# A sixteen-row piece more kept in SBUF by a two-pass channel gate, with the raw rows loaded and stored in another order

## The chip, the cores and the metric

The kernel runs on one core of one Trainium2 chip. The time is the device time of an execution in microseconds; of several runs the median counts. Shares, stretches and chains of waits come from one profiled execution.

## The reference

`x` is 1 x 384 x 384 x 384 in bf16 (113 MB), `w1d` a single weight.

```python
g = jnp.einsum("bhwc->bc", x) / (H * W)      # mean of each channel
s = sigmoid(g * w1d[0])                      # with k = 1 the window is one channel wide
return x * s[:, None, None, :]
```

Every output element needs the mean over the whole input, so `x` is gone through twice: once for the sums, once for the product. It does not fit on the chip.

## The kernel before

**Rows.** A row is one vector of 384 channels in each of the 128 partitions: 768 bytes per partition, 98,304 bytes in all. The input is 1152 rows. One tile, `arena`, holds 275 rows; everything is loaded into it, changed in place and stored from it.

**Kept and streamed rows.** In pass one all 1152 rows are loaded and summed. 785 of them are streamed: summed, overwritten, and loaded again in pass two. 367 are kept in `arena` until the gate is known, more than it has rows, since most are folded: the values of `x` lie in a range in which four exponent bits of each bf16 word are the same in all of them, and the bits of a fourth row are spread over these places in three others. A group of q quads takes 4q loaded rows, of which 3q stay (`GROUPS`, line 168: one of 4, eight of 8 in two columns, and `BANKED`, line 174, of 6, whose folded rows are put into PSUM). 296 kept rows are folded and 71 are raw (`N_RAW`, line 177). A group is worked in pieces of at most 4 quads (`PIECE`), which is 16 rows.

**Fold and unfold.** `fold` (line 292) of a piece first tests the exponent bits: DVE writes the test into scratch Y and ACT sums it into `seen`. Then DVE shifts fields of the fourth row into scratch T and joins them to the three others. Two tests, one after the other, use the same Y. `unfold` (line 470) rebuilds the fourth row with scratch Y in `fields`, restores and scales the three in `three`, and scales the fourth in `fourth`. If a test ever failed, GpSimd would redo the folded rows (`again`, line 540); the trace shows no such work.

**The arena's places.** The two columns of groups, with U (8 rows) and V (8 rows) behind them, which hold the fourth rows of the last groups during the fold; then A, 39 rows, used as three slots S1, S2, S3 of 13 rows; then T (8 rows) and Y (8 rows), the scratch. U, V, the 39 rows of A, T and Y take raw rows at the end of pass one.

**Engines and queues.** SP issues every load and store of rows, in the order of the program, and waits in that order. PE sums rows by a matmul with ones (`sum_rows`, line 253). DVE folds, unfolds and scales; GpSimd scales 13 raw rows in three instructions behind the gate. `Flow` (line 21) gives each operation the waits that its reads and writes of rows demand; a load waits for the sums or stores of what it overwrites.

**End of pass one.** For each group in turn (`BETWEEN`, line 404, and the loop behind it), its rows are loaded, folded and summed while streamed rows pass through the places that are still free, at last through the slots. Then come the raw rows: S2, U, S3, S1, V, Y, and T in two parts. The gate follows on ACT (line 443) and is copied to PSUM for DVE.

**Pass two.** A planner in Python (from line 564) walks a model of the engines in steps of 0.05 us and so fixes the order: which rows DVE scales or unfolds next (`landed`, `turns`), when a store is issued, and when the rows freed by a store are loaded again (`runs`). `landed` starts with the raw rows in a fixed order (line 620): Y, U, T, V, S1, S2. The groups are unfolded in the order `order` (line 634). A group may start when the scratch and its column's places have been stored (`needed`, line 607). Rows of Y, U and V are not given to loads once they are stored, the others are (line 615).

Of the kernel before, what the change touches and what calls it, by code (L numbers as in the profile page):

```python
# [127 lines left out]
def kernel(  # L128
# [25 lines left out]
    PIECE = 4  # L154
    PAIR = 2 * PIECE
    PAIRS = 4
    U = 3 * PIECE + PAIRS * 3 * PAIR
    G0 = U + PAIR
    V = G0 + PAIRS * 3 * PAIR
    A = V + PAIR  # L160
    N_A = 39
    T = A + N_A
    Y = T + 2 * PIECE
    ROWS = Y + 2 * PIECE
# [3 lines left out]
    GROUPS = [(0, PIECE)]  # L168
# [4 lines left out]
            GROUPS.append((a + 3 * PAIR * i, PAIR))  # L173
    BANKED = len(GROUPS)
    GROUPS.append((A, 6))
    PS = 3 * GROUPS[BANKED][1]
    N_RAW = ROWS - V + PAIR
    pool = ctx.enter_context(tc.tile_pool(name="sb", bufs=1))
    psum = ctx.enter_context(tc.tile_pool(name="psum", bufs=1, space=bass.MemoryType.PSUM))

# [15 lines left out]
    BANK = nc.PSUM_BANK_SIZE_BYTES // 2  # L196
    banks = [psum.tile([P, BANK], bf16, name=f"bank{i + 1}") for i in range((PS * C + BANK - 1) // BANK)]

# [6 lines left out]
    def rows(lo, n):  # L205
        return [("a", r) for r in range(lo, lo + n)]
# [4 lines left out]

    N_STREAM = RPP - N_RAW - sum(4 * q for _, q in GROUPS)
    N_KEPT = RPP - N_STREAM
    assert N_STREAM % 2 and N_KEPT % 2
    STREAMED, KEPT = (0, N_STREAM), (N_STREAM, N_KEPT)
# [5 lines left out]
    c_raw = r  # L221
    assert r + N_RAW == N_KEPT

    def raw(a):

        return c_raw + (a - U if a < G0 else PAIR + a - V)


    summed = [0]
# [1 line left out]
    def load(chunk, a, lo, hi):  # L231

        r0, n = chunk
        fl.add(
            "SP",
            lambda: nc.sync.dma_start(out=arena[:, a : a + hi - lo, :], in_=view(xf, r0, n)[:, lo:hi, :]),  # L236
            writes=rows(a, hi - lo), dma=True,
        )
# [14 lines left out]
    def sum_rows(a, n):  # L253
        def emit(i, first, last):
            if first:
                return nc.tensor.matmul(acc, lhsT=ones[:], rhs=arena[:, i, :], start=first, stop=last)  # L256
            return add_held(arena[:, i, :], last)

        for i in range(a, a + n):
            first, last = summed[0] == 0, summed[0] == RPP - 1  # L260
            fl.add(
                "PE", lambda i=i, f=first, l=last: emit(i, f, l),
                reads=[("a", i), "ones"], writes=["bank0"],
            )
            summed[0] += 1
# [7 lines left out]
    def bits(dst, src, op0, s0, op1, s1, reads, writes):  # L273
        fl.add(
            "DVE",
            lambda: nc.vector.tensor_scalar(out=dst, in0=src, scalar1=s0, scalar2=s1, op0=op0, op1=op1),  # L276
            reads=reads, writes=writes,
        )

    def join(dst, a, b, op, reads, writes):  # L280
        fl.add(
            "DVE", lambda: nc.vector.tensor_tensor(out=dst, in0=a, in1=b, op=op), reads=reads, writes=writes  # L282
        )

    def flat(a, p):
        return arena[:, a : a + p, :].bitcast(u16)
# [5 lines left out]
    def fold(k):  # L292

        g, lo, p = pieces[k]
        first, q = GROUPS[g]
        a, ua = first + 3 * lo, first + 3 * q + lo
        wc = [rows(a + j * p, p) for j in range(3)]
        u, uc = flat(ua, p), rows(ua, p)
        t, tc2 = flat(T, 2 * p), rows(T, 2 * p)

        def field(i, op, by, mask):
            bits(flat(T + i * p, p), u, op, by, AND, mask, uc, rows(T + i * p, p))

        def test(i, parts):

            at = Y
            for first, n in parts:
                bits(flat(at, n), flat(first, n), AND, 0x7800, XOR, 0x3800, rows(first, n), rows(at, n))
                at += n
            y = flat(Y, 2 * p)  # L310
            fl.add(
                "ACT",
                lambda: nc.scalar.activation(  # L313
                    out=y, in_=y, func=ACTF.Copy, accum_out=seen[:, 2 * k + i : 2 * k + i + 1]
                ),
                reads=rows(Y, 2 * p), writes=rows(Y, 2 * p) + [("seen", 2 * k + i)],
            )

        test(0, [(a, 2 * p)])
        field(0, SHL, 4, 0x7800)  # L320
        field(1, SHL, 8, 0x7800)
        w01 = flat(a, 2 * p)
        join(w01, w01, t, XOR, wc[0] + wc[1] + tc2, wc[0] + wc[1])
        test(1, [(a + 2 * p, p), (ua, p)])
        field(0, SHL, 12, 0x7000)
        field(1, SHR, 4, 0x0800)
        w2 = flat(a + 2 * p, p)
        for i in range(2):
            join(w2, w2, flat(T + i * p, p), XOR, wc[2] + rows(T + i * p, p), wc[2])
# [17 lines left out]
    streamed = [0]  # L347
# [3 lines left out]
    def stream(n, a):  # L351
        load(STREAMED, a, streamed[0], streamed[0] + n)
        if n > 40 and folding:
            keep_warm(N_WARM)
        sum_rows(a, n)
        streamed[0] += n

    def stream_all(where, n=None):
        i = 0
        n = sum(m for _, m in where) if n is None else n  # L360
        while n:
            a, m = where[i % len(where)]
            m = min(n, m)
            stream(m, a)
            n -= m
            i += 1

    def take(g, lo=0, hi=None):

        a, q = GROUPS[g]  # L370
        hi = 4 * q if hi is None else hi
        load(KEPT, a + lo, c_group[g] + lo, c_group[g] + hi)
        sum_rows(a + lo, hi - lo)

    def of_group(g):
        return [i for i, piece in enumerate(pieces) if piece[0] == g]
# [3 lines left out]
    for k in of_group(BANKED):  # L380
        fold(k)
    in_arena = arena[:, A : A + PS, :].rearrange("p r c -> p (r c)")

    def copy_bank(i, src, dst, reads, writes):
        fl.add(
            "ACT", lambda: nc.scalar.copy(dst.bitcast(u32), src.bitcast(u32)), reads=reads, writes=writes  # L386
        )

    for i, bk in enumerate(banks):
        lo, hi = i * BANK, min((i + 1) * BANK, PS * C)  # L390
        copy_bank(i, in_arena[:, lo:hi], bk[:, 0 : hi - lo], rows(A, PS), [("bank", i)])

    SLOTS = [(A + i, 13) for i in range(0, N_A, 13)]
    S1, S2, S3 = ([slot] for slot in SLOTS)
# [8 lines left out]
    BETWEEN = [  # L403
        LOW_COLUMN, HIGH,
        LOW_COLUMN, [(A, 39)],
        [(G0 - 24, 24), (A - 24, 24)], (S1, S2 + S3),
        (S1, S2 + S3 + S1), (S2, S3 + S1),
    ]
    between = sum(n for b in BETWEEN for w in b for _, n in (w if isinstance(w, list) else [w]))
    first = N_STREAM - between  # L410
    stream_all(EARLY[3:], first % 48)
    stream_all(EARLY, first - first % 48)
# [3 lines left out]
    for g, where in zip(range(1, BANKED), BETWEEN):  # L416
# [6 lines left out]
        else:  # L423
# [4 lines left out]
            take(g, 12, 24)  # L428
            fold(k2)
            stream_all(where[1])  # L430
    assert streamed[0] == N_STREAM

    def take_raw(a, n):
        load(KEPT, a, raw(a), raw(a) + n)
        sum_rows(a, n)

    for a, n in S2 + [(U, 8)] + S3 + S1 + [(V, 8), (Y, 8), (T, 5), (T + 5, 3)]:
        take_raw(a, n)
    assert summed[0] == RPP

# [131 lines left out]
    landed = deque()  # L572
# [31 lines left out]


    SCRATCH = rows(Y, 8)
    needed = [set(SCRATCH + rows(U, 8)), set(SCRATCH + rows(V, 8)), set(SCRATCH)]

    def stored(a, n):

        def f():
            for i in range(a, a + n):
                for left in needed:
                    left.discard(("a", i))
                if not Y <= i < Y + 8 and not U <= i < U + 8 and not V <= i < V + 8:
                    idle[i] = True
        return f


    for a, n, end in ((Y, 4, True), (Y + 4, 4, True), (U, 4, True), (U + 4, 4, True), (T, 8, True), (V, 8, True)):  # L620
        landed.append((KEPT, a, raw(a), n, end))
    for a, n in SLOTS[:2]:
        landed.append((KEPT, a, raw(a), n, True))


    alongside = deque()
# [4 lines left out]
        alongside.append((t, KEPT, a, raw(a), n))  # L631


    order = [g for i in (3, 2) for g in (1 + 2 * i, 2 + 2 * i)] + [BANKED]
    order += [g for i in (1, 0) for g in (1 + 2 * i, 2 + 2 * i)] + [FIRST]
    line = deque(order)
    home = {g: i for i, column in enumerate(COLUMNS) for g in column}
    home[BANKED] = 2
    free = [True, True, True]
    total = len(GROUPS)  # L640
    out_rows = 0
    turns = deque()
# [45 lines left out]
    while True:  # L688

        if dve_at <= now:  # L690
# [4 lines left out]
            if landed and (ahead < PENDING or not can):  # L695
                chunk, a, lo, n, end = landed.popleft()
# [3 lines left out]
                if end or ahead < MERGE:  # L700
                    b, first = since
# [8 lines left out]
        if alongside and alongside[0][0] <= now:  # L710
            _, chunk, a, lo, n = alongside.popleft()
            store(chunk, a, lo, lo + n)
            moves.append([now + LAT, n * ROW + PER_STORE, stored(a, n)])
        while waiting and waiting[0][0] <= now:
            _, n, then, chunk, a, lo, known = waiting.popleft()
# [11 lines left out]
        got = runs()  # L727
        if bank_at is None and len(line) <= total - BANKS_AT and got and max(got)[0] >= PS * 4 // 3:
            a = max(got)[1]
            for i in range(a, a + PS * 4 // 3):  # L730
                idle[i] = False
# [7 lines left out]
        if got and todo < N_STREAM:  # L739
            n, a = max(got)  # L740
            n = min(n, CAP, N_STREAM - todo)
# [52 lines left out]
```

## Time and profile before

| what | value |
|---|---|
| median of 3 runs | 720.82 us (720.63 to 722.88) |
| span of the profiled execution | 719.4 us |
| bytes read / written in HBM | 190.41 / 113.25 MB |
| share of the 16 DMA engines' time taken by packets | 99.0% |
| end of the last sum, gate, first store issued | 268.1, 268.1 to 268.7, 269.7 us |

The span runs from the first to the last instruction of the core; what lies around it, the launch, is not in the trace. The strip over the span shows 40 slices of 18 us: tenths busy for DVE and DMA, and GB/s.

```
DVE  4600004788999719988999998999998985095500
DMA  9999999999999979999999999999999999999997
GB/s 379 435 433 435 426 428 435 438 434 425 426 426 429 427 326 376 421 391 423 430 430 437 430 428 441 428 433 435 430 436 433 429 437 428 441 432 427 440 439 314
```

Slices 15 and 16 hold the seam between the passes. A stretch of the span, as shown further down, can be read for each engine's busy time and for what the DMA engines moved; the chain of waits names, from the end back, what released each step.

### The profile page before, as it was taken

What the parts mean: (1) busy time and instruction counts of PE and PEld (TensorE: products, weight loads), DVE (VectorE), ACT (ScalarE), POOL (GpSimd) and SP (SyncE); (2) the same over time, 40 slices, a digit from 0 to 9 for tenths busy, and PEclk for the clock granted to TensorE, in tenths of its full rate; (3) what the DMA queues carried; (4) which work ended last, traced back from release to release, by engine and by line L of the source; (5) the groups of instructions that cost most, each with busy time, mean ns of one, the idle gap of its engine ahead of it and who ended that gap; (6) DMA issues with size and microseconds to landing.
All of it is one profiled execution on the core that took longest, in us unless ns stands there. A gap on an engine that the chain in (4) does not pass through costs nothing.

```text
span 719.4 us, 2061 instructions
## 1 busy us (share of the span) xinstructions
PE 213.0 (30%) x1202; PEld 0.3 (0%) x3; DVE 493.9 (69%) x471; ACT 115.7 (16%) x93; POOL 10.6 (1%) x7
## 2 busy tenths in 40 slices
PE   4677788897987770000000000000000000000000
PEld 0000000000000000000000000000000000000000
DVE  4600004788999719988999998999998985095500
ACT  3600003566677610002000000000000000000000
POOL 0000000000000005000000000000000000000000
PEclk9899999999999995555555555555555555555555
DMA  9999999999999979999999999999999999999997
GB/s 379 435 433 435 426 428 435 438 434 425 426 426 429 427 326 376 421 391 423 430 430 437 430 428 441 428 433 435 430 436 433 429 437 428 441 432 427 440 439 314
DMA packets 20174, 303.79 MB, mean 422 GB/s; under 512 B 2243, under 2 KB 2243, under 8 KB 6083
## 3 DMA queue, kind: packets, MB, share of 16 engines
q1 hardware_dynamic: 20160, 303.67, 99.0%
q8 instruction: 4, 0.07, 0.0%
q14 instruction: 8, 0.06, 0.0%
q10 hardware_dynamic: 2, 0.00, 0.0%
HBM read 190.41 MB, written 113.25 MB: 422 GB/s over the span
## 4 chain that ended last, share of the span: by engine, by line
DMA 63%; DVE 23%; PE 6%; ACT 2%; another core or an unknown queue 1%; SPq 1%; issue 0%; DVEq 0%
DMA arena<-in_x_dram 42%; DMA out_dram<-arena 20%; DVE arena L456 16%; PE bank L242 6%; DVE arena L276 4%; DVE arena L282 3%; ACT arena L313 2%; SPq L236 1%; ACT s_bf L443 0%; SPq L789 0%; DVEq L112 0%; SPq L106 0%
## 5 line engine op out<-in xcount | busy, mean ns | idle before, releaser
L456 DVE TENSOR_TENSOR arena<-arena,s_bf 128x4608 bf16<-128x4608 bf16 (+8 forms) x97 | 228.7, 2390 | 68.2 <-DMA arena<-in_x_dram 52.2
L276 DVE TENSOR_SCALAR arena<-arena 128x1536 uint16<-128x1536 uint16 (+2 forms) x247 | 145.3, 633 | 111.6 <-DMA arena<-in_x_dram 101.8
L242 PE MATMUL bank<-arena,ones 128*128 128x384 bf16 x1151 | 204.6, 339 | 46.3 <-DMA arena<-in_x_dram 46.3
L313 ACT ACTIVATE arena<-arena 128x3072 uint16<-128x3072 uint16 (+1 forms) x38 | 102.4, 2696 | 142.1 <-DVE arena L276 142.1
L282 DVE TENSOR_TENSOR arena<-arena 128x1536 uint16<-128x1536 uint16 (+2 forms) x114 | 121.0, 1061 | 5.2 <-PE bank L242 2.8
L529 PE MATMUL bank<-odd,ones 128*128 128x1 bf16 x1 | 0.2, 187 | 322.6 <-DVE odd L524 322.6
L456 POOL TENSOR_TENSOR arena<-arena,s_bf 128x1536 bf16<-128x1536 bf16 (+1 forms) x3 | 10.4, 3481 | 268.7 <-ACT bank L447 268.7
L386 ACT COPY arena<-bank 128x512 uint32<-128x512 uint32 (+1 forms) x7 | 4.0, 570 | 58.2 <-DMA out_dram<-arena 58.1
L456 DVE TENSOR_TENSOR arena<-arena,bank 128x1536 bf16<-128x1536 bf16 (+2 forms) x7 | 11.3, 1689 | 0.0
L242 PE MATMUL bank<-zeros,ones 128*128 128x384 bf16 x48 | 8.3, 326 | 0.0
L313 ACT ACTIVATION_READ_ACCUMULATOR arena<-arena 128x1 f32 x38 | 7.1, 186 | 0.0
L386 ACT COPY bank<-arena 128x512 uint32<-128x512 uint32 (+1 forms) x7 | 3.6, 567 | 0.0
L443 ACT ACTIVATE s_bf<-bank,w_sc 128x384 bf16<-128x384 f32 x1 | 0.6, 580 | 14.5 <-PE bank L242 14.5
L256 PE MATMUL bank<-arena,ones 128*128 128x384 bf16 x1 | 0.5, 480 | 6.8 <-DMA arena<-in_x_dram 6.8
L762 ACT ACT_TABLE_LOAD x1 | 1.3, 1283 | 0.7 <-PEq L778 0.7
L343 DVE TENSOR_SCALAR w_sc<-bank 128x1 f32<-128x1 f32 x1 | 0.2, 157 | 1.2 <-PE bank L338 1.2
L333 DVE MEMSET ones<- 128x128 bf16 x1 | 0.2, 165 | 1.0 <-SPq L106 1.0
L338 PE MATMUL bank<-w_bf,ones 1*128 1x1 bf16 x1 | 0.2, 179 | 2.2 <-DMA w_bf<-in_w1d_dram 2.2
L529 PEld LDWEIGHTS bank<-odd,ones 128*128 128x128 bf16 x1 | 0.1, 105 | 581.5 <-DVE odd L524 581.5
L533 DVE CAST odd_i<-bank 128x1 int32<-128x1 f32 x1 | 0.2, 157 | 0.3 <-PE bank L529 0.3
L447 ACT COPY bank<-s_bf 128x192 uint32<-128x192 uint32 x1 | 0.3, 322 | 0.0
L519 DVE TENSOR_REDUCE worst<-seen 128x1 f32<-128x38 f32 x1 | 0.2, 186 | 0.0
(8 smaller groups left out, 0.9 us busy)
## 6 DMA issues: line engine op xcount, KB each, us to landing
arena<-in_x_dram SPq DMA_DIRECT2D x15, 4608.0 KB, 34.8
arena<-in_x_dram SPq DMA_DIRECT2D x21, 1248.0 KB, 13.5
out_dram<-arena SPq DMA_DIRECT2D x7, 3072.0 KB, 33.1
arena<-in_x_dram SPq DMA_DIRECT2D x6, 3072.0 KB, 27.5
out_dram<-arena SPq DMA_DIRECT2D x4, 4608.0 KB, 39.3
arena<-in_x_dram SPq DMA_DIRECT2D x6, 2304.0 KB, 18.5
arena<-in_x_dram SPq DMA_DIRECT2D x3, 4512.0 KB, 27.1
out_dram<-arena SPq DMA_DIRECT2D x10, 1248.0 KB, 11.9
```

Of the source, the lines that this page charges most:

```text
L236: lambda: nc.sync.dma_start(out=arena[:, a : a + hi - lo, :], in_=view(xf, r0, n)[:, lo:hi, :]),
L242: return pe.add_instruction(mybir.InstMatmult(name=nc.get_next_instruction_name(), ins=[pe.lower_ap(rhs), pe.lower_ap(ones[:])], outs=[pe. ...
L256: return nc.tensor.matmul(acc, lhsT=ones[:], rhs=arena[:, i, :], start=first, stop=last)
L276: lambda: nc.vector.tensor_scalar(out=dst, in0=src, scalar1=s0, scalar2=s1, op0=op0, op1=op1),
L282: "DVE", lambda: nc.vector.tensor_tensor(out=dst, in0=a, in1=b, op=op), reads=reads, writes=writes
L313: lambda: nc.scalar.activation(out=y, in_=y, func=ACTF.Copy, accum_out=seen[:, 2 * k + i : 2 * k + i + 1]),
L386: "ACT", lambda: nc.scalar.copy(dst.bitcast(u32), src.bitcast(u32)), reads=reads, writes=writes
L443: lambda: nc.scalar.activation(out=s_bf[:], in_=acc, func=ACTF.Sigmoid, scale=w_sc[:, 0:1]),
L447: "ACT", lambda: nc.scalar.copy(s_ps.bitcast(u32), s_bf[:].bitcast(u32)), reads=["s_bf"], writes=["bank0"]
L456: lambda: vec.tensor_tensor(out=v, in0=v, in1=s[:, None, :].to_broadcast([P, n, C]), op=Op.mult),
L529: lambda: nc.tensor.matmul(votes, lhsT=ones[:], rhs=odd[:], start=True, stop=True),
L762: nc.scalar.preload_act_table(ACTF.Sigmoid)
```

## The change

One more group, `LATE`, of one piece (4 quads, 16 rows) is added. Its 16 rows are loaded into the first 16 rows of A after the eighth group and its streams; 12 stay folded there, and the 4 behind them (D = A + 12) are the fourth rows during the fold. 312 kept rows are now folded and 59 are raw: 371 kept, 781 streamed.

```diff
+    LATE = len(GROUPS)
+    GROUPS.append((A, PIECE))
+    D = A + 3 * PIECE
-    N_RAW = ROWS - V + PAIR
+    N_RAW = 2 * PAIR + ROWS - D
...
-        return c_raw + (a - U if a < G0 else PAIR + a - V)
+        return c_raw + (a - U if a < G0 else PAIR + a - V if a < A else 2 * PAIR + a - D)
```

In pass one the streams through the slots are cut to S1, S2, S3 for each of the last two groups, the late piece follows, then U, nine streamed rows through the rest of S2 (`SPARE`), S3, V, and the last raw loads in falling sizes: 10, 4, 6, 4, 3, 2, 1 rows, of which 4, 6, 4, 3, 2 and 1 lie in D, Y and T.

```diff
-        (S1, S2 + S3 + S1), (S2, S3 + S1),
+        (S1, S2 + S3), (S1, S2 + S3),
     ]
-    between = sum(n for b in BETWEEN for w in b for _, n in (w if isinstance(w, list) else [w]))
+    SPARE = [(D + PIECE, 9)]
+    between = sum(n for b in BETWEEN + [SPARE] for w in b for _, n in (w if isinstance(w, list) else [w]))
...
-    for a, n in S2 + [(U, 8)] + S3 + S1 + [(V, 8), (Y, 8), (T, 5), (T + 5, 3)]:
+    take(LATE)
+    for k in of_group(LATE):
+        fold(k)
+    take_raw(U, 8)
+    stream_all(SPARE)
+    assert streamed[0] == N_STREAM
+
+    for a, n in S3 + [(V, 8), (D + PIECE, 10), (D, PIECE), (Y + 2, 6), (T + 6, 4), (T + 3, 3), (T + 1, 2), (T, 1)]:
         take_raw(a, n)
```

In pass two the raw rows are scaled and stored in the order T, Y, D, U, V and the ten rows behind D; D joins the places that loads do not get; and the late piece is the first to be unfolded, as a fourth column of its own that needs the scratch and D stored.

```diff
-    needed = [set(SCRATCH + rows(U, 8)), set(SCRATCH + rows(V, 8)), set(SCRATCH)]
+    needed = [set(SCRATCH + rows(U, 8)), set(SCRATCH + rows(V, 8)), set(SCRATCH), set(SCRATCH + rows(D, PIECE))]
+    FOURTH = set(rows(U, 8) + rows(V, 8) + rows(D, PIECE) + SCRATCH)
...
-                if not Y <= i < Y + 8 and not U <= i < U + 8 and not V <= i < V + 8:
+                if ("a", i) not in FOURTH:
...
-    for a, n, end in ((Y, 4, True), (Y + 4, 4, True), (U, 4, True), (U + 4, 4, True), (T, 8, True), (V, 8, True)):
+    for a, n, end in ((T, 4, True), (T + 4, 4, True), (Y, 4, True), (Y + 4, 4, True), (D, PIECE, True), (U, 8, True), (V, 8, True), (D + PIECE, 10, True)):
         landed.append((KEPT, a, raw(a), n, end))
-    for a, n in SLOTS[:2]:
-        landed.append((KEPT, a, raw(a), n, True))
...
-    order = [g for i in (3, 2) for g in (1 + 2 * i, 2 + 2 * i)] + [BANKED]
+    order = [LATE] + [g for i in (3, 2) for g in (1 + 2 * i, 2 + 2 * i)] + [BANKED]
...
-    home[BANKED] = 2
-    free = [True, True, True]
+    home[BANKED], home[LATE] = 2, 3
+    free = [True] * 4
```

The planner's constants are unchanged; its order of pass two comes out anew.

More of the change, by code (lines that the diff above doesn't have):

```diff
@@ L430 @@
             stream_all(where[1])
-    assert streamed[0] == N_STREAM
     def take_raw(a, n):
```

## The prediction

> **What bounds the kernel now.** I read the page first (busy shares, the two strips over the span, HBM bytes).
>
> ```profile
> span 719.4 us, 2061 instructions
> PE 213.0 (30%) x1202; PEld 0.3 (0%) x3; DVE 493.9 (69%) x471; ACT 115.7 (16%) x93; POOL 10.6 (1%) x7
> HBM read 190.41 MB, written 113.25 MB: 422 GB/s over the span
> ```
>
> No compute engine is full over the span. The bytes are 1152 rows read in pass one, 785 rows read again and 1152 written (a row is 98,304 B): 3089 rows. Next come stretches of the span: length, busy time of PE, PEld, DVE, ACT and POOL, PE clock, DMA share, GB/s.
>
> ```profile
> 240.00:264.00 24.00, 17.88 (x105) 0.00 (x0) 13.01 (x18) 9.76 (x8) 0.00 (x0) 1.00 1.01 426
> 264.00:272.00 8.00, 3.92 (x24) 0.00 (x0) 3.26 (x4) 0.90 (x2) 2.86 (x1) 1.00 0.39 158
> 272.00:282.00 10.00, 0.00 (x0) 0.00 (x0) 10.00 (x8) 0.00 (x0) 7.52 (x3) 0.52 1.05 430
> 282.00:286.00 4.00, 0.00 (x0) 0.00 (x0) 3.97 (x6) 0.00 (x0) 0.00 (x0) 0.50 0.93 275
> 286.00:312.00 26.00, 0.00 (x0) 0.00 (x0) 23.32 (x20) 0.00 (x0) 0.00 (x0) 0.50 1.01 422
> 312.00:316.00 4.00, 0.00 (x0) 0.00 (x0) 3.97 (x7) 0.00 (x0) 0.00 (x0) 0.50 0.94 274
> 316.00:500.00 184.00, 0.00 (x0) 0.00 (x0) 175.51 (x151) 3.99 (x7) 0.00 (x0) 0.50 1.01 432
> 500.00:714.00 214.00, 0.19 (x1) 0.10 (x1) 135.41 (x88) 0.00 (x0) 0.00 (x0) 0.50 1.00 432
> ```
>
> So the DMA engines set the time: 426 to 432 GB/s nearly everywhere, 98,304 B / 432 GB/s = 0.2276 us per row. They lose time in three places: the seam between the passes (264 to 272 at 158 GB/s: 8 x (432 - 158)/432 = 5.1 us), and two thin stretches, 282 to 286 and 312 to 316 (1.45 us each). The chain of waits shows what the seam is made of.
>
> ```profile
> 253.94 11.35 DMA arena<-in_x_dram
> 265.29 0.04 issue
> 265.33 2.77 PE bank L242 x16
> 268.11 0.02 issue
> 268.13 0.59 ACT s_bf L443
> 268.72 0.02 issue
> 268.74 12.21 DVE arena L456 x8
> ```
>
> The 8-row load of Y lands at 265.29; PE then sums 16 rows in one go (0.173 us each) and the gate follows, then the scaling of raw rows. The issues of this window give the landings of the last two loads (bytes, us to landing).
>
> ```profile
> arena<-in_x_dram SPq DMA_DIRECT2D x1, 480.0 KB, 12.0
> arena<-in_x_dram SPq DMA_DIRECT2D x1, 288.0 KB, 12.2
> ```
>
> They were issued at 254.4 and 254.9 and landed at 266.4 and 267.1. PE ends at 268.1, 1.0 us behind the last landing.
>
> **Part 1, four rows fewer.** Kept rows go from 367 to 371, streamed rows from 785 to 781; pass one still reads all 1152. Pass two loads four rows fewer: 4 x 0.2276 = -0.91 us, on the path, as the DMA share is 1.0 there.
>
> **Part 2, more transfers.** Counted in the order of issues on SP, the loads and stores go from 140 to 153: 49 to 52 in pass one, 91 to 101 in pass two. No row gives the price of a transfer apart from its bytes. Bounds: the last four loads of 8, 8, 5 and 3 rows landed 1.9, 1.2 and 0.7 us after one another where bytes alone take 1.82, 1.14 and 0.68, so the excess is 0 to 0.14 us each (0.14 where a straight line is laid through an 8-row load and a 13-row one, which landed 2.95 us after the one before). I take the middle, 0.07: 13 x 0.07 = +0.91 us (0 to +1.8). A gain is excluded: nothing is merged.
>
> The Trainium skill speaks against this part: DMA: Bandwidth & Descriptors, Anatomy of one DMA, gives every transfer a fixed cost of some 2 us beside its bytes, by which thirteen more would be an estimated +26 us if none of it were hidden. The landings just listed, 0.7 us apart for three rows, do not show it within a full queue.
>
> **Part 3, falling last loads.** The last loads change from V 8, Y 8, T 5, 3 to V 8, then 10, 4, 6, 4, 3, 2, 1 rows. After the 6-row load lands, PE again has 6+4+3+2+1 = 16 rows to sum, 2.77 us. But what is still to land then is 10 rows, not 8: 10 x 0.2276 = 2.28 us, with four prices of 0.07 2.56. PE so ends 0.2 to 0.5 us behind the last landing, not 1.0: -0.6 us (-0.45 to -0.75). SP needs 0.43 us for each of these issues (254.4 to 254.9), longer than one or two rows take, but they go out several us ahead.
>
> **Part 4, the late piece on SP's queue and on DVE in pass one.** Its 16-row load overwrites S1 and the first three rows of S2, so it waits, in order on SP, for PE to sum three rows of S2: 3 x 0.173 = 0.52 us after S2 lands. U, SPARE and all later loads queue behind that wait. First bytes follow an issue by about 0.85 us (store issued at 269.73, engines 73% busy from 270 to 272). That is 1.4 us, and S3's 13 rows (2.96 us) are still running: 1.5 us spare. SPARE's sum (9 x 0.173) plus 0.85 is 2.4 us against 21 rows behind it (4.8 us). The fold takes DVE and ACT 7.7 us (the fold of the last 4-row piece before runs from 245.83 to 253.54); DVE is free, since 42 rows (9.6 us) pass between the landing that this last fold waited for (PE starts on it at 244.89) and the late piece's, 254.4, past 253.54. Behind the late piece 52 rows are queued that do not need the scratch (U 8, SPARE 9, S3 13, V 8, 10, 4): 11.8 us against 7.7 + 0.85 + landing: 2.9 us spare. So I cost it at nothing; cover is the queue itself, and if it failed by a full us each time it would be +1 at LATE and up to 7.7 at Y. ACT's two tests (2.87 us each) end before the gate needs ACT.
>
> **Part 5, pass two on DVE.** Mean times by shape:
>
> ```profile
> L282 DVE TENSOR_TENSOR arena<-arena 128x1536 uint16<-128x1536 uint16 x54 | 51.3, 950 | 0.0
> L276 DVE TENSOR_SCALAR arena<-arena 128x1536 uint16<-128x1536 uint16 x90 | 46.8, 553 | 3.9 <-DMA out_dram<-arena 3.3
> L276 DVE TENSOR_SCALAR arena<-arena 128x4608 uint16<-128x4608 uint16 x18 | 24.3, 1352 | 0.0
> L456 DVE TENSOR_TENSOR arena<-arena,s_bf 128x4608 bf16<-128x4608 bf16 x25 | 63.5, 2551 | 3.8 <-DMA arena<-in_x_dram 3.8
> ```
>
> Unfolding the late piece: 5 x 0.553 + 3 x 0.950 + 1.352 + 2.551 + 0.958 (a 4-row scale) = 10.5 us; it spares scaling 12 raw and 4 streamed rows, about 3.3. Net +7 us on an engine with 8.5 us idle in 316 to 500 and 78 in 500 to 714. But it comes first, where DVE is full. Walk: five 4-row scales, two of 8 and one of 10 take about 9.8 us (58 rows took 12.2): to 278.6. The reload of T has 24 rows ahead of it from 270.55, so lands near 278.2; its scale (1.75) ends at 280.4, the unfolding at 290.9, first bytes 291.8. The engines have by then 67 rows of stores and 39 of loads, 24.1 us, to 294.7. After that come 8 rows (1.75), the next piece's fields (4.1) and a 10-row scale (2.15): 298.9, bytes at 299.8, against a queue that ends at 294.7 + 24 x 0.2276 = 300.1. Spare 0.3 us: covered, barely. I take 0, with 0 to +1.5 as its bounds; below nothing only by rival A.
>
> **Sum.** -0.9 + 0.9 - 0.6 = -0.6 us. Against the profiled execution: span 719.4 to 718.8. The median shown, 720.82, is 1.4 us above that span (launch around it and spread of the runs), so 720.2 us. Own range of this case: all lower ends give -1.7 us, 719.1; the upper ends of parts 2, 3 and 5 give -0.9 + 1.8 - 0.45 + 1.5 = +1.9, 722.7.
>
> **Rivals.** A, faster: the thin stretches vanish. They cost 2.9 us and are the only place in pass two below 420 GB/s. For it: both follow first mixtures of 13-row loads and stores, and the new order has 4 to 10 rows there, with T stored, so reloaded, 5 us sooner. Against it: the DMA share there is 0.93, engines slow rather than empty, which an order need not mend. 720.2 - 2.9 = 717.3.
>
> B, slower: DVE becomes the bound of the first 40 us. The place is the scale of T's reload, which stands before the unfolding on DVE. Before, the first reload (issued at 278.69) took 9.2 us to land. If the new one, issued near 273.7, takes that, DVE idles from 278.6 to 282.9, 4.3 us, has no slack to make it up, and the 10-row store comes 4.3 - 0.3 = 4.0 us too late: 724.2. It decides from 0.3 us of lateness. Against it: that first reload stood behind more rows, and where the engines themselves are slow their queue ends later too.
>
> C: each added transfer pays its whole latency. A lone 4-row store took 2.3 us from issue to landing, 1.4 more than its bytes: 13 x 1.4 = +18, 738. The full queue speaks against it.
>
> D: the piece is not kept, or its rows are read again. The issues of pass two sum to 781 loaded rows, so no.
>
> **Chances.** Forecast 0.53, A 0.27, B 0.18, C 0.01, D 0.01. About 0.3% (2.2 us: 718.7 to 723.0) is what a measurement of this kernel can tell from no change. A falls below it but for its slow end (0.25, and 0.01 of the forecast), B and C above (0.17 and 0.01, and 0.02 of the forecast, where the bounds of parts 2, 4 and 5 add up), all else within: faster 0.26, same 0.54, slower 0.20. The range takes in most of A and the forecast: 717.0 to 723.2.
>
> **What would show it.** Right: 189.9 to 190.1 MB read; PE ends within 0.6 us of the last landing; no gap before the late piece's load or Y's; DVE unbroken from the gate to 290; 430 GB/s or more after 316. Wrong: DVE idle near 278 to 283 followed by a DMA share under 0.9 near 300 (B); both thin stretches gone (A); a DMA share under 0.9 between 240 and 264 (part 4).

## The result and the profile after

Eighteen runs of each kernel have medians of 724.34 us for the changed one (721.85 to 727.61) and 721.94 us for the one before (720.57 to 722.99). The ratio over all runs, which is not that of the medians, is 1.0039, with a 95% interval of 1.0030 to 1.0048. The change makes the kernel slower by 2.4 us by the medians and by some 2.8 us by the ratio (0.39% of 721.9). The forecast was 720.2 us, a small gain, with no change beyond 0.3% the likeliest; the measured time lies outside its range of 717.0 to 723.2, and the change went the other way.

The profiled execution, one of the faster runs of the changed kernel at 723.48 us, has a span of 721.6 us against 719.4. From the page of the changed kernel (span and instructions, busy time of the engines, bytes):

```profile
span 721.6 us, 2100 instructions
PE 212.1 (29%) x1202; PEld 0.3 (0%) x3; DVE 508.7 (70%) x496; ACT 121.4 (17%) x97; POOL 10.6 (1%) x7
HBM read 190.02 MB, written 113.25 MB: 420 GB/s over the span
```

0.39 MB less is read, the four rows, so the piece is kept. Yet the same DMA engines move 420 GB/s instead of 422, and fewer bytes took longer. Where the rate is lost is shown by stretches of the changed kernel's span (start:end, length, busy time of PE, PEld, DVE, ACT, POOL, PE clock, DMA share, GB/s):

```profile
240.00:264.00 24.00, 17.82 (x106) 0.00 (x0) 18.62 (x26) 14.29 (x10) 0.00 (x0) 1.00 0.98 403
244.00:248.00 4.00, 2.41 (x15) 0.00 (x0) 3.77 (x5) 2.86 (x2) 0.00 (x0) 1.00 0.89 316
264.00:272.00 8.00, 4.64 (x28) 0.00 (x0) 2.71 (x4) 0.91 (x2) 2.31 (x1) 0.93 0.51 200
272.00:282.00 10.00, 0.00 (x0) 0.00 (x0) 7.35 (x6) 0.00 (x0) 8.05 (x3) 0.50 1.00 345
276.00:280.00 4.00, 0.00 (x0) 0.00 (x0) 3.10 (x2) 0.00 (x0) 4.00 (x2) 0.50 0.97 246
282.00:286.00 4.00, 0.00 (x0) 0.00 (x0) 3.96 (x6) 0.00 (x0) 0.00 (x0) 0.50 1.03 428
286.00:312.00 26.00, 0.00 (x0) 0.00 (x0) 25.63 (x26) 0.00 (x0) 0.00 (x0) 0.50 1.01 408
312.00:316.00 4.00, 0.00 (x0) 0.00 (x0) 3.96 (x4) 0.00 (x0) 0.00 (x0) 0.50 1.02 427
320.00:450.00 130.00, 0.00 (x0) 0.00 (x0) 123.37 (x111) 4.00 (x7) 0.00 (x0) 0.50 1.01 424
450.00:700.00 250.00, 0.19 (x1) 0.10 (x1) 192.71 (x141) 0.00 (x0) 0.00 (x0) 0.50 1.01 433
```

The same last two stretches, and the one from 244 to 248, of the kernel before:

```profile
244.00:248.00 4.00, 2.60 (x16) 0.00 (x0) 3.73 (x6) 2.97 (x3) 0.00 (x0) 1.00 1.03 439
...
320.00:450.00 130.00, 0.00 (x0) 0.00 (x0) 123.32 (x111) 3.99 (x7) 0.00 (x0) 0.50 1.01 431
450.00:700.00 250.00, 0.19 (x1) 0.10 (x1) 183.59 (x127) 0.00 (x0) 0.00 (x0) 0.50 1.01 433
```

Three things stand out. In pass one there is a new thin place at 244 to 248, 316 GB/s against 439, and 403 against 426 over 240 to 264. The two thin places of pass two (282 to 286 and 312 to 316) are full now, but another has come at 276 to 280, and 286 to 312 has gone from 422 to 408. And from 320 to 450 the rate is 424 instead of 431 at a DMA share of 1.01 in both: the engines are not idle, they are slower at their work. That alone is 130 x (431 - 424)/431 = 2.1 us. Behind 450 both kernels move 433.

The chain of waits of the changed kernel about the end of pass one (start, us, what):

```profile
245.63 6.18 DMA arena<-in_x_dram
251.81 0.04 issue
251.85 5.61 PE bank L245 x33
257.46 0.02 issue
257.48 5.97 DMA arena<-in_x_dram
263.44 0.04 issue
263.49 5.17 PE bank L245 x30
268.65 0.02 issue
268.68 0.59 ACT s_bf L453
```

The late piece's load goes out at 245.63, when PE has summed the rows it overwrites, and lands 6.18 us later; the gate starts at 268.68, before at 268.13. So of the 2.2 us that the span grew, 0.55 lie ahead of the gate and 1.65 behind it, and behind it the four rows should have won 0.91.

One more line, from DVE's timeline of the changed kernel (start, us; in brackets the idle time before it and what ended that):

```profile
281.75 1.76 DVE L466 TENSOR_TENSOR arena<-arena,bank 128x3072 bf16<-128x3072 bf16 x1 [2.65 <-DMA arena<-in_x_dram]
```

This is the scale of T's reload, which stands in front of the unfolding. The reload was issued at 274.39 and took 7.3 us to land, so DVE stood still for 2.65 us. It is the place that the slower rival (B) named, and the prediction had this reload land near 278.2; it landed at 281.7.

### The profile page after: what moved, and what is told of

The parts are those of the page before. It is cut to its first block, busy times and chain, and to the rows that moved or that the text cites. A ratio compares the mean times of both kernels' runs of the same rounds, so it can differ in the third digit from the quotient of the medians.

```text
span 721.6 us, 2100 instructions
## 1 busy us (share of the span) xinstructions
PE 212.1 (29%) x1202; PEld 0.3 (0%) x3; DVE 508.7 (70%) x496; ACT 121.4 (17%) x97; POOL 10.6 (1%) x7
## 2 busy tenths in 40 slices
DMA packets 22045, 303.40 MB, mean 420 GB/s; under 512 B 2450, under 2 KB 2706, under 8 KB 8850
## 3 DMA queue, kind: packets, MB, share of 16 engines
HBM read 190.02 MB, written 113.25 MB: 420 GB/s over the span
## 4 chain that ended last, share of the span: by engine, by line
DMA 64%; DVE 22%; PE 7%; ACT 1%; POOL 1%; SPq 0%; issue 0%
DMA arena<-in_x_dram 48%; DMA out_dram<-arena 16%; DVE arena L466 15%; PE bank L245 7%; DVE arena L279 4%; DVE arena L285 3%; POOL arena L466 1%; ACT arena L316 1%; SPq L239 0%; ACT s_bf L453 0%; ACT bank L457 0%; SPq L798 0%; SPq L106 0%
## 5 line engine op out<-in xcount | busy, mean ns | idle before, releaser
L466 DVE TENSOR_TENSOR arena<-arena,s_bf 128x1536 bf16<-128x1536 bf16 (+8 forms) x102 | 230.4, 2289 | 67.5 <-DMA arena<-in_x_dram 56.9
L279 DVE TENSOR_SCALAR arena<-arena 128x1536 uint16<-128x1536 uint16 (+3 forms) x260 | 153.2, 635 | 107.0 <-DMA arena<-in_x_dram 99.8
L316 ACT ACTIVATE arena<-arena 128x3072 uint16<-128x3072 uint16 (+1 forms) x40 | 108.0, 2700 | 142.4 <-DVE arena L279 142.4
L285 DVE TENSOR_TENSOR arena<-arena 128x1536 uint16<-128x1536 uint16 (+2 forms) x120 | 127.6, 1064 | 5.3 <-PE bank L245 2.7
```

The source lines that it names most:

```text
L316: lambda: nc.scalar.activation(out=y, in_=y, func=ACTF.Copy, accum_out=seen[:, 2 * k + i : 2 * k + i + 1]),
L466: lambda: vec.tensor_tensor(out=v, in0=v, in1=s[:, None, :].to_broadcast([P, n, C]), op=Op.mult),
```

## The experiments

All ratios are to the kernel before, run beside it on the same chip, over all runs as above; intervals are 95%. "Gate" is the start of ACT's work on the gate in the profiled execution (before: 268.13). Two accounts were at hand at first: the late piece's load that waits in pass one, and DVE's wait for T's reload in pass two (rival B); the addresses joined them later.

**The order of the loads, DVE's wait, the last loads.** The changed kernel with U's load ahead of the late piece's:

```diff
+    take_raw(U, 8)
     take(LATE)
     for k in of_group(LATE):
         fold(k)
-    take_raw(U, 8)
```

> The changed kernel with U's raw load (8 rows) issued ahead of the late piece's load instead of behind it, so that 21 rows and not 13 are under way while SP waits for PE to sum three rows of S2. Theory P (that wait empties the DMA engines in pass one; 1.1 us of the +2.4 us come from there): no thin stretch near 244 to 248 us, gate at 267.6 instead of 268.7 us, time 1.1 us under the changed kernel's, ratio to the kernel before 1.0018. Theories Q (DVE waits for T's reload in pass two) and R (price of more and smaller transfers): gate and time as in the changed kernel, ratio 1.0033 to 1.0039.

725.96 us, 1.0056 (1.0043 to 1.0070), gate 269.59. The stretch 244 to 248 was full again (420 GB/s), but the stall had moved to later loads, those of D and behind, and the gate came later still. A miss: in this profile the other order only chose which load waits.

The changed kernel with T stored last, so that no reload stands ahead of the unfolding:

```diff
-    for a, n, end in ((T, 4, True), (T + 4, 4, True), (Y, 4, True), (Y + 4, 4, True), (D, PIECE, True), (U, 8, True), (V, 8, True), (D + PIECE, 10, True)):
+    for a, n, end in ((Y, 4, True), (Y + 4, 4, True), (D, PIECE, True), (U, 4, True), (U + 4, 4, True), (V, 8, True), (D + PIECE, 10, True), (T, 8, True)):
```

> The changed kernel with T stored as the last of the raw rows instead of the first (order Y, D, U, V, ten rows, T), so that DVE reaches the late piece's unfolding without a reload in front of it. Theory Q: no DVE idle between 278 and 283 us, the late piece's store 2 us earlier, and 1.5 to 2.6 us of time gone, ratio to the kernel before 1.000 to 1.0015. Theories P and R: the DVE wait goes but the DMA engines lose as much in the first 50 us of pass two, ratio 1.003 to 1.004.

727.98 us, 1.0086 (1.0072 to 1.0100), gate 268.22. DVE's timeline of this kernel:

```profile
274.83 3.81 DVE L466 TENSOR_TENSOR arena<-arena,bank 128x3840 bf16<-128x3840 bf16 x2
278.56 2.39 DVE L279 TENSOR_SCALAR arena<-arena 128x1536 uint16<-128x1536 uint16 x3
```

The unfolding (the second line) starts at 278.56 with no wait in front of it, 4.9 us sooner than the 283.42 of the changed kernel, and the kernel is slower still. Taking DVE's wait away thus did not bring the time back. (It is not a clean test: the planner's order came out with 162 transfers instead of 153, and the profile is that of the fastest of five runs, 724.41 us where the others took 727.1 to 729.4. Why it lost some 3 us more is not settled.)

The changed kernel with the last loads not falling:

```diff
-... (D, PIECE), (Y + 2, 6), (T + 6, 4), (T + 3, 3), (T + 1, 2), (T, 1)]:
+... (D, PIECE), (Y, 8), (T, 5), (T + 5, 3)]:
```

> The changed kernel with the last raw loads as before (10, 4, 8, 5 and 3 rows instead of 10, 4, 6, 4, 3, 2, 1: two transfers fewer). Prediction's part 3: PE ends 1.0 us instead of 0.4 us behind the last landing, so the gate comes 0.4 to 0.6 us later and the time is +0.4 us over the changed kernel's, ratio 1.0040 to 1.0045. If small last loads cost more than they save (theory R): the same or faster, ratio 1.0033 or less.

726.74 us, 1.0059 (1.0045 to 1.0073), gate 271.01. Beside the changed kernel's two measurements (1.0039 above, 1.0057 below) no difference can be told. The other way round, the kernel before with falling last loads:

```diff
-    ... + [(V, 8), (Y, 8), (T, 5), (T + 5, 3)]:
+    ... + [(V, 8), (Y + 2, 6), (T + 6, 4), (T + 3, 3), (T + 1, 2), (T, 1)]:
```

> The kernel before with only its last loads changed to falling sizes (V 8, then 6, 4, 3, 2, 1 rows in place of 8, 5, 3: two transfers more). Prediction's part 3: gate 0.4 to 0.6 us earlier, ratio 0.9992 to 0.9995. Theory R with 0.2 us or more a transfer: ratio 1.000 or above.

721.57 us beside 721.51, 0.9996 (0.9987 to 1.0005), gate 268.01. Falling loads are worth between a loss of 0.4 and a gain of 0.9 us; the gate itself moved by 0.12.

**The late load's wait cut shorter, the addresses, the room, the transfers.** The changed kernel with S2 of the last group streamed as 3 and 10 rows, so that the late load waits only for the first three, which land before the ten:

```diff
-        (S1, S2 + S3), (S1, S2 + S3),
+        (S1, S2 + S3), (S1, [(A + 13, 3), (A + 16, 10)] + S3),
```

> The changed kernel with one streamed load split: in the last group's streams S2 is loaded as 3 rows and 10 rows, so that the three rows that the late piece overwrites are summed while 23 rows (5.2 us), not 13, are still under way. Theory L (a load stalls the DMA engines by 0.3 to 1.5 us when its data are wanted less than about 4 us after its issue, in pass one as in pass two): no stall on the late piece's load, gate at 267.6 to 268.2 instead of 268.7 us, time 0.5 to 1.1 us under the changed kernel's, ratio to the kernel before 1.002 to 1.003. If the late load's wait costs nothing at the end: 1.0035 to 1.0045.

725.81 us, 1.0065 (1.0052 to 1.0078), gate 269.54. A miss: the late load went out at 244.61, only 1 us sooner; 244 to 248 rose to 382 GB/s, and 258 to 264 fell to 320.

The next one rests on a by-product of the change. Rows are stored in DRAM in two regions, one of streamed and one of kept rows, each laid out so that a partition's rows lie together: partition p starts N_STREAM rows behind partition p - 1 in the one, N_KEPT rows in the other. With 371 kept rows these strides go from 785 and 367 rows to 781 and 371, and with them the address of nearly every row. This kernel is the changed one with the four rows of D put into the streamed region's end, so that the strides are 785 and 367 again; the transfers, their sizes and their order stay:

```diff
-    STREAMED, KEPT = (0, N_STREAM), (N_STREAM, N_KEPT)
+    OWN = N_STREAM + PIECE
+    STREAMED, KEPT = (0, OWN), (OWN, RPP - OWN)
...
+        if D <= a < D + PIECE:
+            return STREAMED, N_STREAM + a - D
+        return KEPT, raw(a) - (PIECE if a >= D + PIECE else 0)
...
```

> The changed kernel with the addresses of the kernel before: the streamed region keeps 785 rows per partition and the kept one 367, and the four raw rows in D come from the streamed region's last four. Same transfers, sizes, order and count of loaded rows. Theory S (the new strides of 781 and 371 rows make HBM slower): ratio 1.000 or below. Theories L and R (short leads, price per transfer): as the changed kernel, 1.003 to 1.006.

722.95 us, 1.0018 (1.0004 to 1.0032), gate 269.96, and 428 GB/s from 320 to 450. Though its gate was over a microsecond later than the changed kernel's, about half of the loss was gone.

The kernel before with 16 of A's rows withheld from reloads for the first 35 us of the plan, as the late piece withholds them:

```diff
+    HOLD, held = 35.0, {i: False for i in range(A, A + 16)}
...
-                    idle[i] = True
+                    if i in held:
+                        held[i] = True
+                    else:
+                        idle[i] = True
...
```

> The kernel before with 16 rows of A withheld from the reloads of the first 35 us of pass two (as the late piece holds them), nothing folded in addition, so 785 rows are streamed. Theory L with too little room in circulation: loads go out later and smaller, their leads are under 4 us more often, ratio 1.002 to 1.004. If the late piece's DVE work or its fold is what costs: 0.999 to 1.001.

723.28 us, 1.0023 (1.0014 to 1.0031), gate 268.31. Its stretches:

```profile
296.00:300.00 4.00, 0.00 (x0) 0.00 (x0) 2.01 (x2) 0.00 (x0) 0.00 (x0) 0.50 0.96 344
300.00:304.00 4.00, 0.00 (x0) 0.00 (x0) 2.96 (x2) 0.00 (x0) 0.00 (x0) 0.50 0.95 390
304.00:308.00 4.00, 0.00 (x0) 0.00 (x0) 4.00 (x4) 0.00 (x0) 0.00 (x0) 0.50 0.95 266
```

Less room in circulation does cost the kernel before 1.7 us, as thin stretches. But the changed kernel moves 445, 414 and 421 GB/s in these three stretches, so this shows what room is worth, not what the change lost.

The kernel before with each reload of 16 rows or more issued as two, 17 transfers more:

```diff
-                load(STREAMED, a, todo, todo + n)
+                half = n // 2 if n >= 16 else n
+                load(STREAMED, a, todo, todo + half)
+                if half < n:
+                    load(STREAMED, a + half, todo + half, todo + n)
```

> The kernel before with every reload of 16 rows or more in pass two issued as two halves at the same place: 17 transfers more, the same rows in the same order, in a queue some 10 us deep. Theory R at 0.07 us a transfer: +1.2 us, ratio 1.0016; at 0.14 us: +2.4 us, 1.003. Theory L (what costs is the short lead, not the number): 1.000 to 1.0008.

722.29 us beside 721.45, 1.0012 (1.0003 to 1.0021): 0.87 us for 17 transfers, 0.05 us each (0.01 to 0.09).

**The addresses again, each way.** The changed kernel as it is, the one with the old strides, and the kernel before with the new strides (781 and 371; four streamed rows are put into the other region, at the price of three transfers), on one chip:

```diff
# the kernel before
+    OWN = N_STREAM - PIECE
+    STREAMED, KEPT = (0, OWN), (OWN, RPP - OWN)
...
```

> The changed kernel itself once more, to stand beside the next three on the same chip. Ratio to the kernel before 1.003 to 1.0065 (the variants with its strides gave 1.0056 to 1.0065 in other calls).

> The changed kernel with the strides of the kernel before (785 and 367 rows), once more, now beside the changed kernel on one chip. Theory S (the strides of 781 and 371 rows cost by themselves): at least 1.0 us under the changed kernel beside it. Without S: within 0.7 us of it.

> The kernel before with the strides of the changed kernel: the streamed region has 781 rows per partition and the kept one 371, and its last four streamed rows come from the kept region's end (three transfers more, nothing else moved). Theory S: +1.5 us or more, ratio 1.002 to 1.004. Without S: +0.2 us for three transfers, 0.9995 to 1.001.

The changed kernel: 725.12 us, 1.0057 (1.0040 to 1.0074). With the old strides: 722.93, 1.0029 (1.0010 to 1.0049). The kernel before with the new strides: 722.17, 1.0008 (0.9998 to 1.0018). The stretch from 320 to 450 of the three, in this order:

```profile
320.00:450.00 130.00, 0.00 (x0) 0.00 (x0) 121.33 (x109) 4.00 (x7) 0.00 (x0) 0.50 1.01 421
```

```profile
320.00:450.00 130.00, 0.00 (x0) 0.00 (x0) 124.16 (x113) 4.00 (x7) 0.00 (x0) 0.50 1.01 428
```

```profile
320.00:450.00 130.00, 0.00 (x0) 0.00 (x0) 122.31 (x109) 3.99 (x7) 0.00 (x0) 0.50 1.01 430
```

The changed kernel gets 7 GB/s back with the old strides, 130 x 7/428 = 2.1 us, the size of the difference of the medians (2.2). The transfers of the kernel before hardly care: 430 with the new strides, 431 without. It takes both, these addresses and the new plan's transfers.

**The late load set free.** First a miss: the old strides, with the late load put between the loads of the eighth group and its fold between that group's folds (the last two groups' streams then leave out the late piece's places, and D and the ten rows behind it are loaded ahead of V).

```diff
+            if g == BANKED - 1:
+                take(LATE)
...
+            if g == BANKED - 1:
+                fold(of_group(LATE)[0])
...
```

> The changed kernel with the old strides and the late piece moved ahead: its load goes out right behind the eighth group's first 20 rows and its fold between that group's two folds, so that 33 rows are under way while it waits for S2 and a whole group's loads stand before the last ones. Theory L for pass one: no stall on its load or the last ones, gate at 267.6 to 268.3 us, and 0.5 to 1.5 us under the kernel with old strides beside it. If pass one's stalls are not what costs: the same as that kernel within 0.4 us.

726.65 us, 1.0069 (1.0054 to 1.0083), gate 273.95, with 429 GB/s from 320 to 450. Other loads now wait, S3's and SPARE's, and longer.

Then the last group's streams are cut so that the late load overwrites 16 rows streamed earlier: behind those, 12 rows of the group and 10 + 13 streamed ones are issued, and are still under way when it goes out. SPARE, not U, comes next; the strides are the old ones, by the edit shown above:

```diff
-        (S1, S2 + S3), (S1, S2 + S3),
+        (S1, S2 + S3), ([(A, 16)], [(A + 16, 10)] + S3),
...
-    take_raw(U, 8)
     stream_all(SPARE)
+    take_raw(U, 8)
```

> The changed kernel with the old strides (785 and 367), the last group's first stream made 16 rows wide over just the rows that the late piece overwrites, so that 35 rows and not 13 are under way behind their sum, and SPARE issued ahead of U. Theory L for pass one: no stall on the late piece's load, gate at 267.6 to 268.3 us, 0.5 to 1.2 us under the kernel with old strides alone (722.9), ratio 1.000 to 1.002. If pass one's extra time is not that wait: gate 268.9 or later, ratio 1.002 to 1.003.

721.55 us beside 721.77, 0.9999 (0.9991 to 1.0008), gate 268.35. With both edits the loss is gone. Three more kernels ask which of the two strides it is: 789 and 363, 781 and 367 (D in a region of its own), 793 and 359, all on the changed kernel with its waiting late load.

```diff
# 789 and 363
+    MOVED = [(V, 8)]
# 781 and 367
+    OWN = N_STREAM
+    STREAMED, KEPT, APART = (0, OWN), (OWN, N_KEPT - PIECE), (RPP - PIECE, PIECE)
# 793 and 359
+    MOVED = [(V, 8), (D, PIECE)]
...
```

> The changed kernel with V's eight raw rows moved to the streamed region, whose stride becomes 789 rows and the kept one's 363; transfers, sizes and order as in the changed kernel. Theory S in its narrow form (785 and 367 are good, others not): pass two loses 8.5 us or more to stalls, ratio to the kernel before 1.004 to 1.0065. If 781 and 371 are the bad ones: pass two loses about 6.8 us as with 785 and 367, ratio 1.001 to 1.003.

> The changed kernel with the kept region's stride back at 367 rows and the streamed one's left at 781; the four rows in D lie in a third region at the end. If the streamed stride is what costs: as the changed kernel, ratio 1.004 to 1.0065, pass two loses 8.5 us or more. If the kept stride: as with both old strides, ratio 1.0015 to 1.003, pass two loses about 6.8 us.

> The changed kernel with V's and D's rows in the streamed region: strides 793 and 359 rows. A second look at how particular the strides are, with the same two cases as 789 and 363: pass two loses 8.5 us or more and 1.004 to 1.0065, or about 6.8 us and 1.001 to 1.003.

| strides | time, us | ratio | gate, us | gate to end of span, us | GB/s, 320 to 450 |
|---|---|---|---|---|---|
| 789, 363 | 724.39 | 1.0039 (1.0024 to 1.0054) | 270.39 | 452.4 | 427 |
| 781, 367 | 723.47 | 1.0023 (1.0012 to 1.0033) | 268.06 | 453.2 | 424 |
| 793, 359 | 724.10 | 1.0037 (1.0025 to 1.0049) | 270.47 | 451.6 | 429 |

By the rate from 320 to 450 it is the streamed region's 781: every kernel with the new plan and 781 shows 418 to 424 there, every one with 785, 789 or 793 shows 427 to 429. The length from the gate to the end says the same: 453.2 us with 781 and 367 is as long as with 781 and 371 (452.9 in the changed kernel), and 785 gives 451.1 and 451.2 in the two kernels above. The whole time does not show it, since 789 and 793 lose in pass one, at a later gate, what they win in pass two.

Last, both settings of the strides with the late load set free, side by side:

```diff
# strides 781 and 371: the edit to the last group's streams, SPARE and U alone
# strides 785 and 367: the same, and the edit that restores the strides
```

> The changed kernel with its own strides (781 and 371) and only the pass-one edit of the kernel above (first stream of the last group 16 rows wide, SPARE ahead of U). If strides and the late piece's wait are two separate costs: pass two still loses 8.5 us or more, gate at 268.0 to 268.6 us, 0.7 to 1.5 us under the changed kernel, ratio 1.002 to 1.0045. If only both together help: ratio 1.004 to 1.0065.

> The kernel with old strides and the late piece's load freed of its wait, once more beside the kernel before on another call: ratio 0.999 to 1.001, pass two loses 6 to 6.8 us. A ratio under 0.9985 would make it a version that beats both.

724.86 us, 1.0047 (1.0035 to 1.0060), gate 267.93, and 721.48 us, 1.0004 (0.9993 to 1.0014), gate 268.13. The stretches of the kernel with 781 and 371:

```profile
240.00:264.00 24.00, 19.26 (x113) 0.00 (x0) 17.78 (x25) 14.28 (x10) 0.00 (x0) 1.00 1.01 421
244.00:248.00 4.00, 2.62 (x16) 0.00 (x0) 3.77 (x7) 2.86 (x2) 0.00 (x0) 1.00 1.01 431
...
286.00:312.00 26.00, 0.00 (x0) 0.00 (x0) 25.35 (x26) 0.00 (x0) 0.00 (x0) 0.50 1.01 409
...
320.00:450.00 130.00, 0.00 (x0) 0.00 (x0) 122.16 (x110) 4.00 (x7) 0.00 (x0) 0.50 1.01 421
```

and of the one with 785 and 367:

```profile
240.00:264.00 24.00, 19.18 (x113) 0.00 (x0) 17.88 (x25) 14.29 (x10) 0.00 (x0) 1.00 1.01 420
...
276.00:280.00 4.00, 0.00 (x0) 0.00 (x0) 2.55 (x2) 0.00 (x0) 3.50 (x1) 0.50 0.96 245
...
286.00:312.00 26.00, 0.00 (x0) 0.00 (x0) 25.59 (x27) 0.00 (x0) 0.00 (x0) 0.50 1.01 416
...
320.00:450.00 130.00, 0.00 (x0) 0.00 (x0) 124.27 (x114) 3.99 (x7) 0.00 (x0) 0.50 1.01 429
```

Pass one is the same in both: the thin place at 244 to 248 is gone. Pass two moves the same transfers at 421 and 429 GB/s, 130 x (429 - 421)/429 = 2.4 us, and at 409 and 416 from 286 to 312, 0.4 us more. The medians of the times lie 3.4 us apart, those of the spans 2.4 (721.9 and 719.5): the five runs with 781 and 371 spend 2.6 us in the median outside the span, where the other kernel and the one before spend 1.8. And DVE's timeline of the second kernel, which is level with the one before:

```profile
280.95 1.75 DVE L474 TENSOR_TENSOR arena<-arena,bank 128x3072 bf16<-128x3072 bf16 x1 [2.40 <-DMA arena<-in_x_dram]
```

The wait for T's reload is there all the same, 2.40 us of it.

**What the four settings give together** (ratio to the kernel before):

| | late load waits | late load set free |
|---|---|---|
| strides 781, 371 | 1.0039 and 1.0057 | 1.0047 |
| strides 785, 367 | 1.0018 and 1.0029 | 0.9999 and 1.0004 |

By these ratios the strides are worth 0.0024 with the wait and 0.0045 without it (means of a cell), 1.7 and 3.2 us. The wait is worth 0.0022, 1.6 us, with the old strides, and nothing that can be told with the new ones. The two seem not to add up, but part of that is the time outside the span named above. By the medians of the spans the strides are worth 2.3 us with the wait (723.25 and 720.95, on one chip) and 2.4 without it. The profiles, split at the gate, show the two costs apart (gate, then gate to the end of the span, in us; 268.1 and 451.3 for the kernel before):

| | late load waits | late load set free |
|---|---|---|
| strides 781, 371 | 268.7, 452.9 and 268.7, 453.5 | 267.9, 453.7 |
| strides 785, 367 | 270.0, 451.1 and 268.9, 451.2 | 268.4, 450.4 and 268.1, 451.4 |

What follows the gate goes with the strides, some 2 us, whether the load waits or not; the gate comes sooner where the load is free, with either setting. Each cell has only one or two kernels on one or two chips. No version tried is faster than the kernel before by more than the noise.

## Why the prediction was wrong

**Part 1, four rows fewer: right in count, wrong in what it left out.** 190.02 MB were read, as forecast. The step that failed is its price: taking 4 x 0.2276 us off the path supposes that the remaining rows move as fast as before. N_STREAM is a row count and also the stride between partitions in DRAM, so the same edit moved the addresses, and from 320 to 450 the rate fell from 431 to 424 (421 in the second profile). "430 GB/s or more after 316" was named as the sign of the forecast; it did not come. No term of the sum and no rival stood for it, and this was the larger part of the error: 1.7 to 3.2 us by the times of the pairs that differ in the strides alone, 2.3 and 2.4 by their spans.

**Part 4, the late piece's load: costed at nothing, and failed.** "1.5 us spare" took S3's 13 rows, 2.96 us, to be still to run when S2 lands. The trace's packets show why they were not. Each transfer ends in 16 packets of 4 bytes (153 x 16 of the 2450 packets under 512 B), read here as one for each DMA engine. Those of S2 come at 242.7 to 243.3 from eleven engines and at 244.1 to 244.6 from five, and S2's landing, at 244.91, follows the last of them. Those of S3 come at 245.7 to 246.3 and 247.1 to 247.5. So when S2 landed, eleven of the 16 engines had only 0.8 to 1.4 us of S3 left, and the late load's first packets start at 246.58, 1.67 us after that landing. The stretch from 244 to 248 lost 4 x (431 - 316)/431 = 1.1 us, 240 to 264 lost 24 x (426 - 403)/426 = 1.3, and the gate came 0.55 us later where part 3 had promised 0.6 sooner. The prediction's "+1 at LATE" was the right price, but it stood on the side of the choice that was not taken. With 35 rows issued between what the load overwrites and the load itself, the stretch is full; 13 were too thin a cover. The sign named for it, a DMA share under 0.9 between 240 and 264, appears only in the short stretch (0.89; 0.98 over the whole), so it was stated too coarsely: GB/s showed the loss where the share hardly did.

**Part 2, more transfers: right.** 0.07 us each was taken; splitting reloads measured 0.05 (0.01 to 0.09), on transfers of 8 rows and more; no run prices the change's own small ones by themselves. The section of the Trainium skill that the prediction named (DMA: Bandwidth & Descriptors, Anatomy of one DMA — SWDGE (gpsimd) path) gives its fixed cost of some 2 us for transfers that GpSimd issues, and puts it down mainly to completion latency; here SP issues. 17 more transfers would be 34 us by it, as an estimate, if none of it were hidden, and cost 0.87.

**Part 3, falling last loads: the mechanism right, the term too large.** The last one-row load landed at 268.2 and PE ended at 268.65, 0.44 us behind it (0.2 to 0.5 forecast). But the edit alone moved the gate of the kernel before by 0.12 us and its time by 0.0004 of 721.5, 0.3 us (interval from a gain of 0.9 to a loss of 0.4), not 0.6. There PE ended 0.56 us behind the last landing instead of 0.97, as meant, but that landing itself came 0.31 us later (267.43 and 267.12), with two transfers more.

**Part 5 and rival B: the wait came, and cost nothing that shows.** T's reload took 7.3 us to land, DVE stood still for 2.65 us (4.3 was rival B's figure), and "DVE unbroken from the gate to 290" was wrong. That B's 724.2 lies beside the measured 724.34 is luck and does not make B right: a kernel with 2.40 us of this wait is level with the one before, and one with none of it is the slowest of all. So B's point of decision, 0.3 us of lateness, was far too tight.

**Rival A** read the thin stretches as something that an order could mend. At 282 and 312 it did, and a new one, 276 to 280 at 246 GB/s, took their place at the first reload of the new order. Moved, not vanished.

**The base.** 720.2 was reckoned from 720.82, the median of three runs; eighteen give 721.94. So 1.1 us of the distance to 724.34 is not the change's.

So the forecast's own terms, with the measured sizes, come to -0.91 + 13 x 0.05 - 0.3 = -0.6 us; the two versions with old strides and a free late load measured -0.1 and +0.3 (0.9999 and 1.0004, their intervals some 0.6 to 0.8 us to either side). The sum is about right for a kernel whose addresses stay and whose late load does not wait; the change as made had two costs, the slower addresses and that wait, which the sum held at nothing.

**Left open.** Why these addresses are slower for the new plan's transfers and not for the old: the trace has the rate of the engines but not where in the memory a row lies. Why the slower rate ends near 450. Why the gate of kernels with the waiting late load varies from 268.1 to 271.0 us: the changed kernel with the old strides, profiled twice, gave 269.96 and 268.94. The gates past 269.5 come with a thin stretch from 258 to 264 (320 to 374 GB/s, where the sooner ones have 409 to 419); what makes it come and go is not shown.

## What to carry to other kernels

When a count in the code is also a stride or an offset in DRAM, a change to the count is two changes: test it with the old layout kept, with transfers and sizes the same. Ask of every load that waits how many bytes are still under way when it goes out, and ask it of the engines that are ahead: a landing tells when the last engine is done, not the first. A stall at the place where a rival put it is not yet its cause: take the stall away alone and see whether the time comes back.

## What the runs showed of the hardware that was not expected

The same transfers, in the same sizes and order, ran 2% apart by address alone. The page's line on packets of the changed kernel is the same whether it has the new strides or the old (from the second profile of the changed kernel; the one with the old strides has this line word for word but for a mean of 421 GB/s):

```profile
DMA packets 22045, 303.40 MB, mean 420 GB/s; under 512 B 2450, under 2 KB 2706, under 8 KB 8850
```

Equal packets of equal sizes, 421 against 428 GB/s over 130 us, a DMA share of 1.01 in both. The share tells that engines have a packet in hand, not how fast it goes: a slow stretch and a full one look alike in it.

The two thin places of the changed kernel differ in kind. In the packets of the trace, those of the late load start 0.96 us after its issue, and until then the engines run out of work, 0.5 us each in the mean: 244 to 248 has a DMA share of 0.89. The packets of the first reload of pass two start 2.4 us after its issue, and 276 to 280 moves 246 and 245 GB/s in the changed kernel and in the version that is level with the one before, at a share of 0.97 and 0.96: there the engines are slow rather than idle. That it is the first reload's own start which makes it thin was not tested by itself.
